# Reordering one stage border of a fused cross-attention and MLP kernel: the last G1 steps of batch 0, an activation-table load, and a W1 piece of batch 1

## The chip, the cores and the metric

The kernel runs on one core of one Trainium2 chip. A core has five engines that run their own instruction queues and meet only at semaphores: TensorE (PE in the profile, its weight loads PEld), VectorE (DVE), ScalarE (ACT), GpSimd (POOL) and SyncE (SP), which here only issues DMAs. The metric is the device time of one launch in microseconds (us), the median of several runs. Positions "at 36.55" are us from the start of the span in the profile of the kernel before.

## The reference, cut to what matters

```python
# x: (8, 8, 512, 64)  state: (8, 8, 32, 64)   B, H, S, D and B, H, Ns, D
scores  = (x @ state^T) / 8;      a  = softmax(scores);   xread = a  @ state    # 512 rows a batch
scores2 = (state @ x^T) / 8;      a2 = softmax(scores2);  sread = a2 @ x        # 32 rows a batch
t   = concat([xread, sread], axis=2)        # -> (8 * 544, 512), heads side by side
h   = t @ w_in                              # w_in (512, 2048)
out = (h * sigmoid(h)) @ w_out              # w_out (2048, 512), float32 result of 4352 x 512
```

The kernel leaves out the subtraction of the row maximum, which changes nothing in a softmax of such small scores.

## The kernel before, in words

**The algebra.** For the 512 x-rows of a batch `b`, `xread @ w_in` is `a @ (state @ w_in)`. So the kernel makes `W1[b] = state[b] @ w_in` (256 rows, one for each head and state, by 2048 columns) and multiplies the normalised softmax `aT[b]` with it; `xread` itself is never formed. The 32 sread rows of all eight batches are gathered and go through the MLP at the end as a "batch" 8 of their own.

**The steps of a batch, and their names.**
- `cast_x` converts x to bf16; `pe_transpose_x` (line 243) transposes it on TensorE through a PSUM bank, and a copy on the engine given in `engs` takes it to `xT`. Batches 0 and 1 do it this way; later batches use DMA transposes.
- `scores` (L304) and `exps` (L318): scores into PSUM, the exponential on ScalarE. `hg` 0 and 1 are the two halves of the heads.
- `norm` (L377 row sums, L378 reciprocal, both on VectorE; L380 product, on GpSimd for `hg` 0 and on VectorE for `hg` 1), then `pe_transpose_a` (L396): transposes the probabilities to `aT`.
- W1 in pieces of up to 512 columns: `w1_mms` (L464, eight small matmuls for each half of a PSUM pair) and `w1_out` (copies to bf16 `W1`, L156 on ScalarE or L158 on VectorE). A half-batch is one PSUM bank, so a 512-column piece needs two banks.
- G1 step `k` (L518, `emit_G1`): two matmuls of 512 columns, one for each `hg`, and a SILU on ScalarE (L550) that gives the tile `g` number `k`; batch `b` has the steps `16 b` to `16 b + 15`. `upto(n)` emits all steps below `n` that are not emitted yet. The two PSUM buffers of tag `h1` hold the G1 results, so step `k` cannot start before the SILU of step `k-2` has read its buffer.
- G2 (L559): one matmul of 512 columns that adds `g` number `ft` times `w_out` into one of the four output tiles `tt` of a batch; `store` copies a finished output tile to SBUF and writes it out.

**What sets the order.** The scheduler is switched off (`tc.manual_schedule()`); every engine runs its instructions in the order in which the program emits them, and a wait holds up all that stands behind it on its engine. The order around the change is written out by hand in lines 604 to 720. Lines 604 to 645 are the start: attention of batch 0, with dummy matmuls (`keep_busy`, L164) between. Lines 650 to 679 are a loop over `ft` 0 to 11 of batch 0 in which G1 runs `LEAD0[ft]` steps ahead (but not past `ready`, the W1 columns made so far), W1 pieces of batch 0 (`W0`) and batch 1 (`W1_AT`) are put in, and then G2 for `tt` 0 to 2, with some of `tt` 3. Lines 680 to 720 are the border to batch 1: the rest of G2 of batch 0 lies between the steps of the softmax of batch 1.

**Activation tables.** ScalarE holds one table at a time: the exponential and SILU take turns, with a table load between (`ACT_TABLE_LOAD`). Lines 686 and 700 are one-element activations (`warm`) that pull such a load to a chosen place: 686 ahead of the exponentials of batch 1, 700 back to SILU for its G1 steps.

**PSUM.** Eight banks: `o0`, `o1` (pool psO), two buffers `h1` (psH), `a0` to `a3` (psA). In batch 0 the output tiles `tt` 0 to 3 lie in `o0`, `o1`, `a0`, `a1`; `bank` gives the a-banks named in `banks` in turn, in the border only `a2` and `a3` at first.

The loop and the border of the kernel before, cut to what the change touches:

```python
    W0 = {2: (512, 512), 6: (1024, 512), 10: (1536, 512)}
    W1_AT = {4: 0, 6: 512, 10: 1024}
    LEAD0 = [2, 2, 2, 2, 2, 3, 2, 1, 3, 3, 2, 1]
...
    nc.scalar.activation(warm[:], busy[:, 0:1], func=EXP, bias=0.0)
    for ft in range(8, 11):
        G2(0, 3, ft)
    scores(1, 0, new=new_h)
    G2(0, 3, 11)
    scores(1, 1, new=new_h)
    exps(1, 0)
    exps(1, 1)
```

Of the kernel before, what the change touches and what calls it, by code (L numbers as in the profile page):

```python
# [14 lines left out]
EXP = mybir.ActivationFunctionType.Exp  # L15
# [26 lines left out]
def kernel(  # L42
# [8 lines left out]
    nc = tc.nc  # L51
# [14 lines left out]
    psO = ctx.enter_context(tc.tile_pool(name="psO", bufs=1, space=bass.MemoryType.PSUM))  # L66
    psH = ctx.enter_context(tc.tile_pool(name="psH", bufs=2, space=bass.MemoryType.PSUM))
    psA = ctx.enter_context(tc.tile_pool(name="psA", bufs=1, space=bass.MemoryType.PSUM))
# [38 lines left out]
    def load_x(b, h0=0, nh=H, eng=nc.gpsimd):  # L107
        eng.dma_start(
            x_f[b % 2][:, ds(h0, nh)],
            x[b, ds(h0, nh)].rearrange("h (p c) d -> p h c d", p=128, c=4)  # L110
        )
# [42 lines left out]
    def copy(eng, dst, src):  # L154
        if eng is nc.scalar:
            nc.scalar.activation(dst, src, func=COPY, bias=0.0)  # L156
        else:
            eng.tensor_copy(dst, src)  # L158


    def keep_busy(n, pool, tag):
        ps = pool.tile([128, 512], FP32, tag=tag, name="ps_busy")
        for _ in range(n):
            nc.tensor.matmul(  # L164
                ps[:], busy[:, 0:128], busy[:], start=True, stop=True, skip_group_check=True
            )

    warm = pers.tile([128, 1], FP32)
    busy = pers.tile([128, 512], BF16)
# [26 lines left out]
    both = (nc.vector, nc.scalar)  # L196
# [46 lines left out]
    def pe_transpose_x(b, hg, nb=2, new=bank, engs=(nc.vector, nc.scalar), only=None):  # L243
        if b not in xT:
            xT[b] = xtpool.tile([128, 4, 4, 128], BF16, tag="xT", name=f"xT{b}")
        m = 4 // nb
        for u in range(nb) if only is None else only:
            ps = new([128, m, 2, 128], BF16, "ps_xt")
            for i in range(m):
                for j in range(2):  # L250
                    nc.tensor.transpose(  # L251
                        ps[:, i, j, :],
                        x_nat[b][:, m * u + i, 2 * hg + j, :],
                        ident[:],
                    )
            copy(engs[u], xT[b][:, ds(m * u, m), ds(2 * hg, 2), :], ps[:])
# [41 lines left out]
    def scores(b, hg, m=4, new=bank):  # L298
        sc_ps[hg] = []
        for c in range(4):  # L300
            if c % m == 0:
                sc_ps[hg].append(new([128, m, 4, NS], FP32, "ps_sc"))
            for j in range(2):
                nc.tensor.matmul(  # L304
                    sc_ps[hg][-1][:, c % m, ds(2 * j, 2), :],
                    xT[b][:, c, 2 * hg + j, :],
                    stT[:, b, 2 * hg + j, :, :],
                    start=True,
                    stop=True,
                    skip_group_check=True,  # L310
                )
# [141 lines left out]
    def w1_mms(b, cols, new=bank):  # L453
        pss = {}
        if b not in W1:
            W1[b] = wpool.tile([128, 2, DF], BF16, tag="W1", name="W1")
        for f, n in cols:
            for hg in range(2):
                pss[f, hg] = new([128, 512], FP32, "ps_w1")
            for s in range(4):  # L460
                for hg in range(2):
                    h = HEAD_OF_SLOT[hg][s]
                    r = 64 * (h % 2)
                    nc.tensor.matmul(  # L464
                        pss[f, hg][ds(32 * s, 32), 0:n],
                        stT[ds(r, 64), b, h // 2, s % 2, :],
                        w_in_sb[ds(r, 64), h // 2, ds(f, n)],
                        start=True,
                        stop=True,
                        tile_position=(r, 32 * s),  # L470
                        skip_group_check=True,
                    )
        return pss

    def w1_out(b, cols, engs, pss, at=0):
        for f, n in cols:
            for hg in range(2):
                copy(engs[hg], W1[b][:, hg, ds(f + at, n)], pss[f, hg][:, ds(at, n)])

    def w1_cols(b, cols, engs, new=bank):  # L480
        w1_out(b, cols, engs, w1_mms(b, cols, new))
# [45 lines left out]
    def emit_G1(k):  # L527
        b, ft = divmod(k, NFT)
        if b < B:
            if k == 0:  # L530
                g1_first()
                return
            g1_half(k, 0)
            g1_half(k, 1)
            ps = h_ps.pop(k)
        else:
            ps = psH.tile([128, 512], FP32, tag="h1", name="h1")
            for kt in range(4):
                nc.tensor.matmul(  # L539
                    ps[:, 0:256],  # L540
                    w_in_sb[:, kt, ds(128 * ft, 128)],
                    xmT[:, :, kt].rearrange("p t n b -> p t (n b)"),
                    start=(kt == 0),
                    stop=(kt == 3),
                    skip_group_check=True,
                )
        n = 512 if b < B else 256
        g = gpool.tile([128, 512], BF16, tag="g", name="g")
        gt[k] = g
        nc.scalar.activation(g[:, 0:n], ps[:, 0:n], func=SILU, bias=0.0)  # L550

    def G2(b, tt, ft):
        if ft == 0:
            if b == 0 and tt >= 2:
                outs[tt] = psA.tile([128, DM], FP32, tag=f"a{tt - 2}", name="o_a")
            else:
                i = (tt + (b > 0)) % 2 if tt < 3 else 0
                outs[tt] = psO.tile([128, DM], FP32, tag=f"o{i}", name="o")
        nc.tensor.matmul(  # L559
            outs[tt][:],  # L560
            gt[b * NFT + ft][:, ds(128 * tt, 128)],
            w_out_sb[:, ft, :],
            start=(ft == 0),
            stop=(ft == NFT - 1),
            skip_group_check=True,
        )

    def store(b, tt, eng):
        o = opool.tile([128, DM], FP32, tag="o_sb", name="o_sb")
        copy(eng, o[:], outs[tt][:])  # L570
        if b < B:
            nc.sync.dma_start(out_re[ds(136 * b, 128), tt, :], o[:])
        else:
            nc.sync.dma_start(out_sread[ds(512, 32), ds(4 * tt, 4), :], o[:])
# [21 lines left out]
    def upto(k):  # L596
        while done[0] < min(k, (B + 1) * NFT):
            emit_G1(done[0])
            done[0] += 1

    new_h = lambda sh, dt, nm: psH.tile(sh, dt, tag="h1", name=nm)
# [2 lines left out]
    scores(0, 0)  # L604
    exps(0, 0)
    keep_busy(1, psH, "h1")
    pe_transpose_x(0, 1, 2, new_h, (nc.vector, nc.vector))
    norm(0, 0)
    scores(0, 1, 2)
    exps(0, 1)  # L610
# [38 lines left out]

    turn[0] = 0  # L650
    W0 = {2: (512, 512), 6: (1024, 512), 10: (1536, 512)}
    W1_AT = {4: 0, 6: 512, 10: 1024}
    LEAD0 = [2, 2, 2, 2, 2, 3, 2, 1, 3, 3, 2, 1]
    T3 = {1: (0, 1), 2: (2,), 3: (3,), 4: (4,), 5: (5,), 6: (6,)}
    ready = 4
    for ft in range(12):
        upto(min(ft + LEAD0[ft], ready))
        if ft == 1:
            place_one_state(1, transpose_one_state(st1_n), nc.vector)
        if ft in W0:  # L660
            pss = w1_mms(0, [W0[ft]])
            if ft in W1_AT:
                pss1 = w1_mms(1, [(W1_AT[ft], 512)], new_h)
            w1_out(0, [W0[ft]], both, pss)
            if ft in W1_AT:
                w1_out(1, [(W1_AT[ft], 512)], both, pss1)
            ready = sum(W0[ft]) // 128
        elif ft in W1_AT:
            w1_cols(1, [(W1_AT[ft], 512)], both)
        if ft == 11:  # L670
            for hg in range(2):
                cast_x(1, nc.vector, 0, 4, 4 * hg, 4)
            load_x(3)
        for tt in range(3):
            G2(0, tt, ft)
            if ft == 7 and tt == 0:
                upto(9)
        for i in T3.get(ft, ()):
            G2(0, 3, i)
    upto(14)  # L680
    G2(0, 3, 7)
    pe_transpose_x(1, 0, 1, engs=(nc.vector,))
    upto(15)
    pe_transpose_x(1, 1, 1, engs=(nc.vector,))
    upto(16)
    nc.scalar.activation(warm[:], busy[:, 0:1], func=EXP, bias=0.0)
    for ft in range(8, 11):
        G2(0, 3, ft)
    scores(1, 0, new=new_h)
    G2(0, 3, 11)  # L690
    scores(1, 1, new=new_h)
    exps(1, 0)
    exps(1, 1)
# [12 lines left out]
    G2(0, 3, 13)  # L706
    banks[:] = ["a2", "a3", "a0", "a1"]
    turn[0] = 0
    w1_cols(1, [(1536, 512)], (nc.vector, nc.vector))
    store(0, 1, nc.vector)  # L710
    for i in (2, 3):
        for c in range(4):
            cast_x(i, nc.gpsimd, c, 1)
# [108 lines left out]
```

The softmax here doesn't subtract the row's maximum and nothing guards it: scores larger than these inputs give would overflow.

## Time and profile before

| what | value |
| --- | --- |
| time, median of 3 runs | 216.12 us (216.08 to 216.12) |
| profiled span | 214.3 us, 3868 instructions |
| one 512-column matmul of G1 or G2, from one start to the next | 0.216 us (two take 0.43 us in the chain) |
| one SILU of 128 x 512 on ScalarE | 0.596 us |
| ACT_TABLE_LOAD | 1.283 us |
| W1 copy of 128 x 512, VectorE / ScalarE | 0.685 / 0.592 us |

The page of the profile gives busy times by engine, a strip of the span in 40 slices, DMA queues, the chain of work that ended last, and the costliest groups. The chain is read backwards from the last instruction: at each step it goes to what released that instruction, or to the instruction ahead of it on its engine. "Issue" is time in which the engine waited for nothing that the profile shows. The timeline lists instructions in order of time, merged while they are alike, and in square brackets the idle time of the engine ahead of an instruction and what ended it. The end of a matmul is modelled and overlaps the next by about 0.16 us, so on TensorE the distance from start to start is the thing to read.

### The profile page before, as it was taken

How to read it: one execution, taken by the hardware profiler on the slowest of the kernel's cores; microseconds unless marked ns; L12 is line 12 of the kernel's file. 1: busy time of each engine (PE TensorE's matmuls, PEld its weight loads, DVE VectorE, ACT ScalarE, POOL GpSimd, SP SyncE). 2: the span in 40 equal slices, each digit the busy share in tenths (PEclk: the TensorE clock that was granted, in tenths of full speed). 3: DMA queues.
4: the chain of work that ended last, by engine and by line, in shares of the span. 5: the costliest groups of instructions: out<-in, count | busy, mean ns of one | idle time of the engine just before them, and what ended most of it. 6: DMA issues, size and time to landing. Idle time of an engine off the chain costs nothing.

```text
span 214.3 us, 3868 instructions
## 1 busy us (share of the span) xinstructions
PE 205.3 (96%) x1549; PEld 97.0 (45%) x1575; DVE 76.7 (36%) x171; ACT 139.3 (65%) x244; POOL 39.9 (19%) x62
## 2 busy tenths in 40 slices
PE   7899998999899999999999999999999999999993
PEld 2443354445344444444444444444444444466653
DVE  3752275566951156106610651135312415200011
ACT  3766669699567876698559956886675366644410
POOL 8592213702420312003100402000200000000000
PEclk9999999999999999999999999999999999999999
DMA  6999999497649548464657483114310211011112
GB/s 200 191 205 206 292 268 345 123 251 246 83 97 272 159 109 195 98 198 104 180 68 245 77 178 100 49 52 104 97 50 22 85 49 54 0 49 49 52 49 98
DMA packets 42930, 28.66 MB, mean 134 GB/s; under 512 B 28064, under 2 KB 37792, under 8 KB 42912
## 3 DMA queue, kind: packets, MB, share of 16 engines
q1 hardware_dynamic: 36720, 20.65, 36.6%
q0 software_dynamic: 5904, 7.64, 17.2%
q8 instruction: 12, 0.20, 0.4%
q10 hardware_dynamic: 288, 0.13, 0.2%
q14 instruction: 6, 0.05, 0.1%
HBM read 17.43 MB, written 8.91 MB: 123 GB/s over the span
## 4 chain that ended last, share of the span: by engine, by line
PE 88%; DVE 6%; ACT 3%; issue 1%; POOL 0%
PE o L559 47%; PE h L518 25%; PE ps_w L464 4%; PE h L539 3%; PE o_a L559 2%; PE ps_busy L164 2%; PE o_part L581 2%; DVE rs L377 1%; DVE W L158 1%; PE ps_sr L416 1%; DVE rc L432 1%; PE ps_xt L251 1%; DVE an L380 1%; DVE xT L158 1%; ACT exp_nat L318 1%
## 5 line engine op out<-in xcount | busy, mean ns | idle before, releaser
L559 PE MATMUL o<-w_out_sb,g 128*128 128x512 bf16 x486 | 130.0, 379 | 1.7 <-issue 0.9
L550 ACT ACTIVATE g<-h 128x512 bf16<-128x512 f32 (+1 forms) x143 | 81.4, 573 | 36.9 <-PE h L518 21.8
L559 PEld LDWEIGHTS <-g 128*128 128x128 bf16 x528 | 50.2, 98 | 58.2 <-issue 3.5
L518 PE MATMUL h<-aT,W 128*128 128x512 bf16 x241 | 72.0, 379 | 0.1
L158 DVE COPY o_sb<-o 128x512 f32<-128x512 f32 x15 | 10.4, 691 | 87.7 <-PE o L559 80.2
L518 PEld LDWEIGHTS <-W 128*128 128x128 bf16 x254 | 24.5, 98 | 29.9 <-issue 1.0
L158 DVE CAST W<-ps_w 128x512 bf16<-128x512 f32 (+2 forms) x35 | 22.1, 658 | 26.4 <-PE ps_w L464 26.4
L156 ACT ACTIVATE W<-ps_w 128x512 bf16<-128x512 f32 (+1 forms) x33 | 17.1, 562 | 12.6 <-PE ps_w L464 12.6
L158 POOL CAST x_nat<-x_f 128x512 bf16<-128x512 f32 x24 | 14.6, 650 | 31.7 <-issue 21.7
L156 ACT ACTIVATE o_sb<-o 128x512 f32<-128x512 f32 x16 | 9.5, 596 | 12.1 <-PE o L559 8.9
L360 POOL TENSOR_TENSOR an<-e,rcn 128x512 bf16<-128x512 bf16 x5 | 7.6, 1518 | 51.0 <-DVE rcn L358 51.0
L464 PE MATMUL ps_w<-w_in_sb,stT 64*32 64x512 bf16 (+2 forms) x264 | 10.8, 375 | 0.8 <-DVE W L158 0.7
L539 PE MATMUL h<-xmT,w_in_sb 128*128 128x256 bf16 x64 | 9.6, 273 | 0.0
L559 PE MATMUL o_a<-w_out_sb,g 128*128 128x512 bf16 x30 | 9.6, 379 | 0.0
L539 PEld LDWEIGHTS <-w_in_sb 128*128 128x128 bf16 x64 | 6.3, 98 | 3.9
L164 PE MATMUL ps_busy<-busy 128*128 128x512 bf16 x15 | 6.4, 533 | 1.2 <-DVE warm L171 1.2
L766 ACT ACT_TABLE_LOAD x5 | 6.4, 1283 | 0.1
L344 ACT ACTIVATE eT<-ps_scT 128x512 bf16<-128x512 f32 x10 | 5.4, 595 | 1.6 <-PE ps_scT L330 1.6
L380 POOL TENSOR_TENSOR an<-exp_nat,rc 128x512 bf16<-128x512 bf16 x3 | 3.1, 1046 | 17.8 <-DMA x_f<-in_x_dram 10.6
L464 PEld LDWEIGHTS <-stT 64*32 64x32 bf16 x264 | 3.2, 89 | 7.0 <-issue 5.1
L357 DVE TENSOR_REDUCE rs<-e 128x32 f32<-128x1024 bf16 x5 | 6.1, 1211 | 0.6 <-DMA e<-eT 0.6
L432 DVE RECIPROCAL rc<-ps_sr 32x2 f32<-32x2 f32 x32 | 5.2, 164 | 0.3
(75 smaller groups left out, 104.1 us busy)
## 6 DMA issues: line engine op xcount, KB each, us to landing
out_dram<-o_sb SPq DMA_DIRECT2D x33, 256.0 KB, 2.4
x_f<-in_x_dram SPq DMA_DIRECT2D x4, 1024.0 KB, 5.8
x_f<-in_x_dram POOLq DMA_DIRECT2D x2, 1024.0 KB, 11.1
w_in_sb<-in_moe_w_in_dram POOLq DMA_DIRECT2D x3, 512.0 KB, 9.6
x_f<-in_x_dram SPq DMA_DIRECT2D x2, 512.0 KB, 4.7
w_out_sb<-in_moe_w_out_dram POOLq DMA_DIRECT2D x4, 256.0 KB, 11.5
w_out_sb<-in_moe_w_out_dram POOLq DMA_DIRECT2D x2, 512.0 KB, 11.4
x_f<-in_x_dram POOLq DMA_DIRECT2D x2, 512.0 KB, 14.2
```

The costliest lines, as they stand in the source:

```text
L156: nc.scalar.activation(dst, src, func=COPY, bias=0.0)
L158: eng.tensor_copy(dst, src)
L164: nc.tensor.matmul(ps[:], busy[:, 0:128], busy[:], start=True, stop=True, skip_group_check=True)
L357: nc.vector.tensor_reduce(rs[:], e2[b][:], axis=AX, op=ADD)
L360: eng.tensor_tensor(a[:, hg], e2[b][:, hg], rc[:, hg].to_broadcast([128, 4, 4, NS]), op=MULT)
L432: nc.vector.reciprocal(rc[q, :], src)
L464: nc.tensor.matmul(pss[f, hg][ds(32 * s, 32), 0:n], stT[ds(r, 64), b, h // 2, s % 2, :], w_in_sb[ds(r, 64), h // 2, ds(f, n)], start=True, ...
L518: nc.tensor.matmul(h_ps[k][:], W1[b][:, hg, ds(128 * ft, 128)], aT[b][:, hg, :, :], start=(hg == 0), stop=(hg == 1), skip_group_check=True,)
L539: nc.tensor.matmul(ps[:, 0:256], w_in_sb[:, kt, ds(128 * ft, 128)], xmT[:, :, kt].rearrange("p t n b -> p t (n b)"), start=(kt == 0), stop ...
L550: nc.scalar.activation(g[:, 0:n], ps[:, 0:n], func=SILU, bias=0.0)
L559: nc.tensor.matmul(outs[tt][:], gt[b * NFT + ft][:, ds(128 * tt, 128)], w_out_sb[:, ft, :], start=(ft == 0), stop=(ft == NFT - 1), skip_gr ...
L766: nc.scalar.activation(warm[:], busy[:, 0:1], func=SILU, bias=0.0)
```

## The change

It does three things.
- **At the start:** the second half of the second transpose of x of batch 0 (`hg` 1) is copied out of PSUM by ScalarE instead of VectorE, so the two copies can run side by side.
- **At the end of the loop of batch 0:** the last W1 piece of batch 0 is made alone at `ft` 10 (the W1 piece of batch 1 that stood beside it, columns 1024 to 1535, goes out). Then `ft` 11 emits the G1 steps 12 and 13 right away (lead 3), casts x of batch 1, transposes its first half, emits the steps 14 and 15 and asks for the exponential table, all ahead of the G2 steps of `ft` 11. The second transpose follows those G2 steps. It is meant to get ScalarE through with SILU of batch 0 earlier, so that the exponentials of batch 1 and what hangs on them come earlier.
- **In the border:** the two last W1 pieces of batch 1 are made in one group, all four banks copied out by VectorE. As four banks are needed at once, a list of its own (`tail_bank`) takes `a2`, `a3`, `a0` and `o0`, the latter two those of the output tiles 2 and 0 of batch 0, which ScalarE has stored by then. The store of output tile 1 moves ahead of the group.

```diff
-    pe_transpose_x(0, 1, 2, new_h, (nc.vector, nc.vector))
+    pe_transpose_x(0, 1, 2, new_h, both)
...
-    W1_AT = {4: 0, 6: 512, 10: 1024}
-    LEAD0 = [2, 2, 2, 2, 2, 3, 2, 1, 3, 3, 2, 1]
+    W1_AT = {4: 0, 6: 512}
+    LEAD0 = [2, 2, 2, 2, 2, 3, 2, 1, 3, 3, 2, 3]
...
             load_x(3)
+            pe_transpose_x(1, 0, 1, engs=(nc.vector,))
+            upto(16)
+            nc.scalar.activation(warm[:], busy[:, 0:1], func=EXP, bias=0.0)
         for tt in range(3):
             G2(0, tt, ft)
...
-    upto(14)
+    pe_transpose_x(1, 1, 1, engs=(nc.vector,))
     G2(0, 3, 7)
-    pe_transpose_x(1, 0, 1, engs=(nc.vector,))
-    upto(15)
-    pe_transpose_x(1, 1, 1, engs=(nc.vector,))
-    upto(16)
-    nc.scalar.activation(warm[:], busy[:, 0:1], func=EXP, bias=0.0)
-    for ft in range(8, 11):
+    scores(1, 0, new=new_h)
+    for ft in range(8, 12):
         G2(0, 3, ft)
-    scores(1, 0, new=new_h)
-    G2(0, 3, 11)
     scores(1, 1, new=new_h)
...
     turn[0] = 0
-    w1_cols(1, [(1536, 512)], (nc.vector, nc.vector))
+    tail_tags = ["a2", "a3", "a0", "o0"]
+
+    def tail_bank(shape, dtype, name):
+        tag = tail_tags.pop(0)
+        return (psO if tag == "o0" else psA).tile(shape, dtype, tag=tag, name=name)
+
     store(0, 1, nc.vector)
+    w1_cols(1, [(1024, 512), (1536, 512)], (nc.vector, nc.vector), tail_bank)
```

## The prediction

> **What bounds the kernel now.** I read the page first: which engine is busy, and whose work is the chain that ended last.
>
> ```profile
> PE 205.3 (96%) x1549; PEld 97.0 (45%) x1575; DVE 76.7 (36%) x171; ACT 139.3 (65%) x244; POOL 39.9 (19%) x62
> ...
> PE 88%; DVE 6%; ACT 3%; issue 1%; POOL 0%
> ```
>
> TensorE is busy for 96% of the span and is 88% of the chain. The change neither adds nor takes a matmul, so it can only win or lose where TensorE stands still. Second I asked the timeline of TensorE for gaps between 26 and 42 us, where the diff moves things:
>
> ```profile
> 36.55 0.40 PE L396 MATMUL ps_at<-ident,an 128*128 128x128 bf16 x4 [0.97 <-POOL an L380]
> 36.79 0.38 PE L559 MATMUL o_a<-w_out_sb,g 128*128 128x512 bf16 x1
> 37.10 0.40 PE L396 MATMUL ps_at<-ident,an 128*128 128x128 bf16 x4
> 37.65 0.41 PE L464 MATMUL ps_w<-w_in_sb,stT 64*32 64x512 bf16 x8
> 37.99 1.04 PE L518 MATMUL h<-aT,W 128*128 128x512 bf16 x4
> ...
> 40.58 0.59 PE L518 MATMUL h<-aT,W 128*128 128x512 bf16 x2
> ```
>
> The one real gap is ahead of 36.55. The twelve G2 steps before it started at 32.83; at 0.216 us they are through at 35.42, so 1.13 us are lost there. The second transpose, at 37.10, could have started at 36.79 + 0.216 = 37.00: 0.10 us more. What put the transpose at 36.55 is told by the chain in the same window:
>
> ```profile
> 31.70 0.60 ACT g L550
> ...
> 32.32 1.28 ACT L686
> ...
> 33.61 0.20 ACT warm L686
> 33.82 0.97 ACT exp_nat L318 x2
> 34.79 0.58 ACT o_sb L156
> ...
> 35.46 1.05 POOL an L380
> ...
> 36.55 0.40 PE ps_at L396 x4
> ```
>
> The last SILU of batch 0, the table load, the exponentials, the product on GpSimd. The step "o_sb" is the profile's guess: line 380 reads only exp_nat and the reciprocal rc. The timeline of VectorE has rc at 35.05 for 0.25, ending 0.16 us before GpSimd starts; the same 0.16 to 0.17 us lie there at 9.62 and 52.01. So the chain is exp, rs (34.33, 0.69), rc, product, and it hangs on the table load at 32.32.
>
> Third, the start of the kernel, in the chain:
>
> ```profile
> 7.83 0.76 DVE xT L158 x2
> 8.59 0.61 DVE rs L377
> ...
> 9.47 0.61 DVE rs L377 x2
> ...
> 10.38 0.84 DVE an L380
> ...
> 11.94 0.49 PE h L502 x3
> ```
>
> and in the timeline of ScalarE:
>
> ```profile
> 8.64 0.71 ACT L318 ACTIVATE exp_nat<-ps_sc 128x256 bf16<-128x256 f32 x2 [0.65 <-PE ps_sc L304]
> ```
>
> Here VectorE is the chain: two copies of xT, then everything of the softmax, while ScalarE has 0.65 us free ahead of 8.64 (its exponential at 7.39 ends at 7.99).
>
> **What the Trainium skill says.** "ScalarE: Activation LUTs", section What ACT_TABLE_LOAD costs: about 1283 ns for the load and about 1380 ns of drain. The load agrees (1.28 us); the drain does not show here: warm starts at 33.61, right behind the load, and the exponential at 33.72. I use 1.40 us from load to exponential. The same section gives an ACTIVATE with immediates 186 ns + 0.833 ns an element, 612 ns for 512, whatever the type; the trace has 0.384 for 256 and 0.591 to 0.597 for 512. "PSUM — Partial Sum Buffer", section Engine vs sequencer instructions: the queues of ScalarE, VectorE and GpSimd are strictly first in, first out. The trace agrees: every engine follows the program text, so a moved line really moves all that stands behind it.
>
> **Part 1, the copy at the start.** The trace has no 128x512 bf16 PSUM copy on ScalarE. Bounds: 0.59 us (its 512-column rows) and 0.63 us (its cast of x); I take 0.60. The second four transposes end near 8.02, so the copy runs 8.04 to 8.65, where VectorE ended the same copy at 8.59: the second half of the scores comes 0.05 us later, the last exponential ends at 9.39 instead of 9.35, and this costs nothing else on ScalarE (table load at 9.75 instead of 9.71). On VectorE, rs starts at 8.16 instead of 8.50, rc at 8.87, the first half sum at 9.04, the second at 9.41 (it waits for that exponential; before 9.68), rc at 9.83, product at 10.11 instead of 10.38. Gain 0.27 us; bounds 0 and 0.34 (the copy's whole step). It reaches TensorE: the dummy matmuls end near 10.5, the transpose that waited for the product moves from 11.28 to 11.01, ScalarE's part of aT (11.2 to 11.6) is in time for L502 at 11.67. No load catches it: the nearest, the w_in columns from 512, landed at 5.0 + 9.6 = 14.6 and are used at 15.52; the one of columns 1536 at 12.2 + 13.1 = 25.3, used at 26.80.
>
> **Part 2, the loop's end,** on the clock of before (all of it 0.27 earlier if part 1 holds). TensorE at 26.80: eight W1 matmuls instead of sixteen, 0.34 instead of 0.56 us (the eight are added back in part 3). Three G2 steps to 27.79. G1 step 12 needs the new W1 piece: at `ft` 2 the same order took 1.23 us from the first W1 matmul (15.52) to G1 (16.75), so step 12 starts at 28.03. **A new wait of 0.24 us**, with G1 12 to 15 and the table load queued behind it. Steps 12, 13 to 28.90; eight transposes to 29.34 (the cast of x ends at 28.6 for this half; its second half waits for x at 28.2 and ends at 29.25, with only the xT copy behind it on VectorE); step 14 to 29.77. Step 15 waits for the SILU of 13: SILU starts 0.64 us after the first matmul of a pair of steps (37.99 to 38.63), so 28.67, and the second ends at 29.75: step 15 at 29.80 to 30.23. Its SILU runs 30.52 to 31.12; the table load comes at **31.13 instead of 32.32**. TensorE: three G2 to 30.88, transposes to 31.32, one G2, scores (xT was copied by 30.2), four G2, scores, at 32.86: where it was before (32.83). Twelve G2 to 35.45.
>
> ScalarE: exponentials at 31.13 + 1.40 = 32.53 and 33.07. VectorE and GpSimd keep their distances, 1.19 us earlier: product on GpSimd ends at 35.3, on VectorE at 35.85. TensorE reaches the first transpose at 35.45, after the product: **the 1.13 us are gone**, with 0.1 to 0.15 us to spare. G2 to 35.90; the second transpose finds its product just ready: 0 to 0.05 lost. G2, and W1 at 36.46.
>
> **Part 3, the border.** Sixteen W1 matmuls, 0.56 us: to 37.02. Their banks are free: a2 and a3 since the xT copies (32.2), o0 and a0 with the stores on ScalarE, which follow the G2 steps and not the exponentials, and end by 35.4 and 35.9. G1 16 needs aT (copied by 36.8), so it starts at 37.02 instead of 37.99. ScalarE's SILU table: load behind those stores at 35.9, ready at 37.4; the first SILU is wanted at 37.66. From G1 16 to G1 20 the trace has 2.59 us, which the SILUs set; kept, 20 starts at 39.61 instead of 40.58. Gain **0.97 us**, less 0 to 0.1 for the tight product: 0.93. VectorE: the store of tile 1 (36.75 to 37.4) ahead of G2 of batch 1 at 39.2; then four copies at 0.645 us to 40.0, where before two copies and a store ended at 40.01. They cost nothing on the path: G1 24 wants the columns from 1024 near 42.2, G1 28 those from 1536 near 44.8. The state transposes wait on SP for the store of tile 1 and get earlier too. From 41.2 on TensorE is solid, and the later steps hang on each other, not on a clock.
>
> **Sum:** 0.27 + 0.93 = 1.20; 216.12 - 1.20 = **214.9 us**.
>
> **Rivals.**
> - *Both parts hold* (0.55): 214.9, 214.7 to 215.1 with the bounds of the copy (0 to 0.34) and the tight product.
> - *Only the border gains* (0.17): the copy on ScalarE pushes the exponentials behind it, and VectorE then waits for them. For it: it takes the same 0.65 us gap almost whole. 216.12 - 0.93 = 215.2.
> - *A wait in place of the one removed* (0.13): step 12 or the SILUs of 12 to 15 come later by half a us (x landing at 28.2, buffers h1), and the product is late again by that much: 216.12 - 0.6 = 215.5. Against: the cast of the first half does not need the late load, and the SILU distances are measured.
> - *No change* (0.07): the chain to the product keeps its place, the front gain pays for the new wait: 216.1.
> - *Slower* (0.08): neither gain, the 0.24 us at step 12 are new: 216.36; and if VectorE's two additional copies (1.29 us) hold up its work for batch 2, up to 217. For it: VectorE carries the whole group of four. Against: it has 3.1 us idle ahead of 43.73.
>
> **Range and chances.** Low 214.5: the 214.7 above, and 0.2 if the SILU-bound stretch of G1 16 to 20 also loosens. High 215.7, which takes in the first three cases. Faster by over 0.2%: 0.85; within: 0.07; slower: 0.08.
>
> **What would show it.** In the profile after: no gap over 0.1 us ahead of the L396 transposes of batch 1; table load of the exponential about 1.2 us (with the front 1.45) earlier; 0.2 us of wait at G1 12 for a DVE copy of W; one group of sixteen L464 near 36.2; L502 near 11.67; the product of batch 0 on VectorE near 10.1. I am wrong if TensorE waits anew at G1 14 or 15, for GpSimd at the transpose, or for VectorE around G1 24, or if the gain at G1 20 is lost again by 60 us.

## The result, and the profile after

The changed kernel takes 214.8 us (median of four runs, 214.54 to 215.1) against 216.1 us before: a ratio of 0.994, 95% interval 0.9923 to 0.9958. Run again beside experiments it took 214.71 us against 216.06 (0.9938, 0.9923 to 0.9952).

For the reading, three marks on TensorE are enough. **S** is the start of the second group of x transposes of batch 0 (L251), the last thing ahead of the copy that the change moves. **M** is the first matmul of the last W1 group of the loop (26.80 us before). **G1 20** is the fifth G1 step of batch 1 (40.58 us before). From S to M only the front part can act, from M to G1 20 only the border part; some of the expectations call this second distance D.

First the page. TensorE's share of the span rose from 96 to 97%, and its share of the chain from 88 to 90%:

```profile
span 212.8 us, 3896 instructions
...
PE 206.4 (97%) x1575; PEld 96.6 (45%) x1575; DVE 77.0 (36%) x171; ACT 139.4 (66%) x244; POOL 39.9 (19%) x62
...
PE 90%; DVE 4%; DMA 2%; ACT 2%; issue 0%; SPq 0%
```

Its higher busy time is not more work: the program has as many matmuls as before (PEld counts 1575 weight loads in both), and the trace of before has 1549 of them, that of after all 1575.

The timeline of TensorE in the border. A row gives the start and the length. A bracket would give the idle time that is left behind the modelled end of the matmul ahead, and there is none in the whole stretch; a shorter wait shows only in the distance from start to start:

```profile
26.24 0.41 PE L464 MATMUL ps_w<-w_in_sb,stT 64*32 64x512 bf16 x8
...
27.02 0.38 PE L559 MATMUL o_a<-w_out_sb,g 128*128 128x512 bf16 x1
27.46 1.04 PE L518 MATMUL h<-aT,W 128*128 128x512 bf16 x4
...
34.47 0.59 PE L559 MATMUL o<-w_out_sb,g 128*128 128x512 bf16 x2
34.90 0.39 PE L396 MATMUL ps_at<-ident,an 128*128 128x128 bf16 x4
35.12 0.38 PE L559 MATMUL o_a<-w_out_sb,g 128*128 128x512 bf16 x1
35.34 0.39 PE L396 MATMUL ps_at<-ident,an 128*128 128x128 bf16 x4
...
35.87 0.63 PE L464 MATMUL ps_w<-w_in_sb,stT 64*32 64x512 bf16 x16
36.43 1.04 PE L518 MATMUL h<-aT,W 128*128 128x512 bf16 x4
...
39.01 0.59 PE L518 MATMUL h<-aT,W 128*128 128x512 bf16 x2
```

The 0.97 us of idle time ahead of the first L396 row are gone: the two transposes start at 34.90 and 35.34, each just when the G2 steps ahead of it are through (34.47 + 0.43 and 35.12 + 0.22). M to G1 20 is 39.01 - 26.24 = 12.77 us; before it was 40.58 - 26.80 = 13.78. Next, ScalarE, GpSimd and VectorE in the timeline of all engines:

```profile
30.52 1.28 ACT L676 ACT_TABLE_LOAD   x1
...
31.92 1.19 ACT L318 ACTIVATE exp_nat<-ps_sc 128x512 bf16<-128x512 f32 x2
...
33.65 1.04 POOL L380 TENSOR_TENSOR an<-exp_nat,rc 128x512 bf16<-128x512 bf16 x1 [3.73 <-DVE rc L378]
...
34.37 0.88 DVE L380 TENSOR_TENSOR an<-exp_nat,rc 128x512 bf16<-128x512 bf16 x1
```

Counted from M, the table load stands at 4.28 us instead of 5.52. GpSimd's product is ready at 34.69, and TensorE only comes for it at 34.90. The profile now also names the reciprocal rc as the releaser, not the store that it named before.

The start, in the timeline:

```profile
7.17 0.61 PE L251 MATMUL ps_xt<-ident,x_rows 128*128 128x128 bf16 x8
7.59 0.43 DVE L158 COPY xT<-ps_xt 128x512 bf16<-128x512 bf16 x1 [0.46 <-PE ps_xt L251]
7.82 0.60 ACT L156 ACTIVATE xT<-ps_xt 128x512 bf16<-128x512 bf16 x1
7.93 0.68 DVE L377 TENSOR_REDUCE rs<-exp_nat 128x16 f32<-128x512 bf16 x1
...
9.05 1.05 POOL L380 TENSOR_TENSOR an<-exp_nat,rc 128x512 bf16<-128x512 bf16 x1 [2.06 <-DVE rc L378]
...
9.95 0.70 DVE L380 TENSOR_TENSOR an<-exp_nat,rc 128x512 bf16<-128x512 bf16 x1
...
11.37 0.20 PEld L502 LDWEIGHTS <-W 128*128 128x128 bf16 x2 [0.27 <-issue]
```

The two copies (7.59 on VectorE, 7.82 on ScalarE) run side by side. From S (7.17) to the second L502 weight load it is 4.20 us; before it was 11.94 - 7.41 = 4.53. But M came 0.56 us earlier than in the first profile of before, which is more than these 0.33: S itself stood 0.24 us earlier, and nothing ahead of S was changed. That asked for an experiment.

### The profile page after: what moved, and what is told of

Its sections match the earlier page's. It is cut to its first block, busy times and chain, and to the rows that moved or that the text cites. A ratio compares the mean times of both kernels' runs of the same rounds, so it can differ in the third digit from the quotient of the medians.

```text
span 212.8 us, 3896 instructions
## 1 busy us (share of the span) xinstructions
PE 206.4 (97%) x1575; PEld 96.6 (45%) x1575; DVE 77.0 (36%) x171; ACT 139.4 (66%) x244; POOL 39.9 (19%) x62
## 4 chain that ended last, share of the span: by engine, by line
PE 90%; DVE 4%; DMA 2%; ACT 2%; issue 0%; SPq 0%
PE o L559 48%; PE h L518 26%; PE ps_w L464 4%; PE h L539 3%; PE o_a L559 3%; DMA x_f<-in_x_dram 2%; PE o_part L581 2%; DVE W L158 1%; PE ps_sr L416 1%; DVE rc L432 1%; PE ps_scT L330 1%; PE ps_busy L164 1%; ACT L318 1%; DVE rs L377 1%; ACT exp_nat L318 1%; PE ps_at L396 0%
## 5 line engine op out<-in xcount | busy, mean ns | idle before, releaser
L559 PE MATMUL o<-w_out_sb,g 128*128 128x512 bf16 x496 | 132.2, 379 | 0.0
L518 PE MATMUL h<-aT,W 128*128 128x512 bf16 x254 | 74.7, 379 | 0.1
L158 DVE CAST W<-ps_w 128x512 bf16<-128x512 f32 (+2 forms) x36 | 22.7, 658 | 26.3 <-PE ps_w L464 26.3
L156 ACT ACTIVATE W<-ps_w 128x512 bf16<-128x512 f32 (+1 forms) x32 | 16.6, 561 | 12.6 <-PE ps_w L464 12.6
L464 PE MATMUL ps_w<-w_in_sb,stT 64*32 64x512 bf16 (+2 forms) x264 | 10.8, 375 | 0.7 <-DVE W L158 0.7
L164 PE MATMUL ps_busy<-busy 128*128 128x512 bf16 x16 | 5.9, 487 | 1.2 <-DVE warm L171 1.2
L380 POOL TENSOR_TENSOR an<-exp_nat,rc 128x512 bf16<-128x512 bf16 x3 | 3.1, 1047 | 15.7 <-ACT eT L344 9.9
## 6 DMA issues: line engine op xcount, KB each, us to landing
x_f<-in_x_dram POOLq DMA_DIRECT2D x2, 512.0 KB, 14.6
```

The lines of the kernel that those rows point to most:

```text
L164: nc.tensor.matmul(ps[:], busy[:, 0:128], busy[:], start=True, stop=True, skip_group_check=True)
L464: nc.tensor.matmul(pss[f, hg][ds(32 * s, 32), 0:n], stT[ds(r, 64), b, h // 2, s % 2, :], w_in_sb[ds(r, 64), h // 2, ds(f, n)], start=True, ...
L518: nc.tensor.matmul(h_ps[k][:], W1[b][:, hg, ds(128 * ft, 128)], aT[b][:, hg, :, :], start=(hg == 0), stop=(hg == 1), skip_group_check=True,)
L559: nc.tensor.matmul(outs[tt][:], gt[b * NFT + ft][:, ds(128 * tt, 128)], w_out_sb[:, ft, :], start=(ft == 0), stop=(ft == NFT - 1), skip_gr ...
```

## The experiments

My theory was that of the prediction: two independent gains, one in the start and one in the border, and in the border one cause, the place of the G1 steps ahead of the table load. The rivals were that the start's gain is luck, that the W1 piece or the explicit table request does it, and that the new wait at G1 step 12 could have been avoided.

### The two halves alone, and both kernels again

The first kernel has one line of the change, the second all the others:

```diff
 front only, on the kernel before
-    pe_transpose_x(0, 1, 2, new_h, (nc.vector, nc.vector))
+    pe_transpose_x(0, 1, 2, new_h, both)

 border only, on the changed kernel
-    pe_transpose_x(0, 1, 2, new_h, both)
+    pe_transpose_x(0, 1, 2, new_h, (nc.vector, nc.vector))
```

> The kernel before with the one edit at the start: ScalarE copies the second half of the second transpose of x of batch 0. My theory: the softmax chain of batch 0 on VectorE gets 0.27 us shorter (0 to 0.34), so the first matmul of the last W1 piece of batch 0 starts near 26.5 instead of 26.80 and the time is about 215.8. From that matmul to G1 step 20 the distance stays 13.78 us. Rival: the 0.56 us that the profile of the changed kernel shows at that mark is luck of the start of that one execution (the clock of TensorE, the landing of x) and has nothing to do with the copy: time 216.1, mark at 26.8.

> The changed kernel with the copy at the start put back on VectorE. My theory: the border alone brings what it brought together with the front: from the last W1 group of the loop to G1 step 20 12.8 us instead of 13.78, time 215.1 to 215.2, and as steady as the kernel before (spread under 0.1). Rival: the border needs the earlier start or shares its gain with it: time 215.5 or more. A third: the spread of 0.56 us between the runs of the changed kernel comes from the border, then it is seen here too.

> The changed kernel once more, for a second profile of it beside the two halves on the same chip. My theory: median 214.8, runs from 214.5 to 215.1; the border again 12.8 us from the last W1 group to G1 step 20, and the start between 26.2 and 26.6 at that W1 group: the spread sits in the first 12 us. Rival: the start is the same 26.24 and the spread sits later.

> The kernel before, one more look at its start. If the first 8 us differ from its first profile in the pace of the transposes and dummy matmuls on TensorE between 4.4 and 6.6, the start of each execution has its own luck; the mark at 26.80 should not move by more than 0.1, since its times lie within 0.05 us. Rival: the mark moves by some 0.3 us as in the changed kernel.

| kernel | time, us | ratio to before | S | S to second L502 load | M | M to G1 20 |
| --- | --- | --- | --- | --- | --- | --- |
| before, first profile | 216.12 | | 7.41 | 4.53 | 26.80 | 13.78 |
| before, again | 215.88 | | 7.17 | 4.54 | 26.58 | 13.77 |
| front only | 215.67 | 0.9977 (0.9966 to 0.9988) | 7.71 | 4.20 | 26.78 | 13.78 |
| border only | 215.15 | 0.9951 (0.9933 to 0.997) | 7.16 | 4.55 | 26.57 | 12.78 |
| changed | 214.8 | 0.994 (0.9923 to 0.9958) | 7.17 | 4.20 | 26.24 | 12.77 |
| changed, again | 214.71 | 0.9938 (0.9923 to 0.9952) | 7.19 | 4.21 | 26.42 | 12.77 |

The two gains are independent and add up: against 216.06 us in that series the front alone brings 0.39, the border alone 0.91, both 1.35. In the columns of distances it is sharper: 0.33 us from S to L502 and 1.0 us from M to G1 20, each only where its half of the change is in.

The other columns tell where most of the spread comes from. S wanders from 7.16 to 7.71 us with no regard to the change, and what the program does ahead of S is the same in all six profiles: it waits for x to land (its first cast on ScalarE starts between 4.97 and 5.27) and runs the first transposes. So my expectation that the mark at 26.80 would be steady in the kernel before was wrong: in its second profile it is 26.58. With the front alone it is 26.78 and not near 26.5, as S was late there (7.71). Nor does the border alone run within 0.1 us: its runs lie between 214.82 and 215.40. One part of the spread lies later. From S to M it is 19.39 to 19.41 us in the three profiles without the front and 19.07 in two with it, but 19.23 in the second profile of the changed kernel; a load of `w_in` is the reason (below, "No load catches it"). So a single profile of such a kernel must be read in distances, not in places.

### The request for the table

```diff
             upto(16)
-            nc.scalar.activation(warm[:], busy[:, 0:1], func=EXP, bias=0.0)
```

> The changed kernel without the one-element exponential that asks for the table behind G1 step 15; the load is left to the exponentials themselves. D is the distance on TensorE from the first matmul of the last W1 group of the loop to G1 step 20: 13.78 us before, 12.77 after. My theory: a load waits for nothing, and ScalarE takes its queue in order, so it comes right behind the SILU of step 15 in either case: D 12.77, time 214.7. What brings the load early is the place of the G1 steps. Rival: without the request the load stays with the exponential and waits with it for the scores, 0.8 us later; then the product is late and D is 13.3, time 215.2.

It took 214.82 us, M to G1 20 is 12.78. ScalarE's timeline of this run:

```profile
31.05 1.28 ACT L318 ACT_TABLE_LOAD   x1
32.35 1.29 ACT L318 ACTIVATE exp_nat<-ps_sc 128x512 bf16<-128x512 f32 x2
```

M is at 26.77 here, so the load comes 4.28 us behind it, just where it comes with the request. It does not wait for the input of its exponential: the scores start on TensorE only at 31.51 in this run, 0.46 us after the load. So the request does no work at this place. It even holds up the first exponential a little: without it that starts 1.30 us behind the start of the load, with it 1.40. Nothing hangs on this 0.1 us here, the distance is 12.78 and 12.77. The rival falls.

### The G1 steps 14 and 15 put back

```diff
             pe_transpose_x(1, 0, 1, engs=(nc.vector,))
-            upto(16)
-            nc.scalar.activation(warm[:], busy[:, 0:1], func=EXP, bias=0.0)
         for tt in range(3):
...
     pe_transpose_x(1, 1, 1, engs=(nc.vector,))
     G2(0, 3, 7)
+    upto(16)
+    nc.scalar.activation(warm[:], busy[:, 0:1], func=EXP, bias=0.0)
     scores(1, 0, new=new_h)
```

> The changed kernel with G1 steps 14 and 15 and the request for the table put back behind the second transpose of x and the G2 step that follows it; the lead of steps 12 and 13 and the W1 group of two pieces stay. My theory: ScalarE gets to the table load some 1.3 us later, GpSimd's product is late again, TensorE waits about 1.1 us ahead of the first transpose of the probabilities, D is 13.8 and the time 215.7. Rival: the gain comes from the W1 piece or from the steps 12 and 13, and D stays near 12.9.

It took 216.09 us (ratio 0.9988, 0.9977 to 0.9999): with these two steps late nearly the whole gain is gone, and the border is worse than before (M at 26.58, G1 20 at 40.64: 14.06 us). The timeline of TensorE:

```profile
31.71 0.39 PE L304 MATMUL ps_sc<-stT,xT 128*128 128x64 bf16 x8 [0.25 <-ACT g L550]
...
36.41 0.40 PE L396 MATMUL ps_at<-ident,an 128*128 128x128 bf16 x4 [0.62 <-POOL an L380]
```

The wait for GpSimd is back, as expected, and with it the cause is shown: the request alone moved nothing in the run above, so it is the place of these two steps. (The early steps 12 and 13 were not tried alone.) The other wait I had not expected: the scores take a G1 buffer, and right behind G1 14 and 15 both buffers still wait for their SILUs, so TensorE stands 0.25 us ahead of the scores. It costs nothing: the exponential starts 1.40 us behind its table load all the same (32.17 and 33.57), and TensorE waits for the product afterwards. That the distance is 14.06 and not 13.8 has another reason, which I had not counted: the eight W1 matmuls that the change moved now stand behind the wait for the product and not ahead of it. From the first transpose to G1 16 it is 1.64 us here and 1.44 before. The rest is the product itself, 8.72 us behind M instead of 8.66.

### The W1 piece: left in place, and moved alone

```diff
 left in place, on the changed kernel
-    W1_AT = {4: 0, 6: 512}
+    W1_AT = {4: 0, 6: 512, 10: 1024}
...
-    w1_cols(1, [(1024, 512), (1536, 512)], (nc.vector, nc.vector), tail_bank)
+    w1_cols(1, [(1536, 512)], (nc.vector, nc.vector), tail_bank)

 moved alone, on the kernel before (with tail_tags and tail_bank as in the change)
-    W1_AT = {4: 0, 6: 512, 10: 1024}
+    W1_AT = {4: 0, 6: 512}
...
-    w1_cols(1, [(1536, 512)], (nc.vector, nc.vector))
-    store(0, 1, nc.vector)
+    store(0, 1, nc.vector)
+    w1_cols(1, [(1024, 512), (1536, 512)], (nc.vector, nc.vector), tail_bank)
```

> The changed kernel with the W1 piece of batch 1 (columns 1024 to 1535) left where it was, beside the last piece of batch 0; all else as in the change. My theory: this piece lies in the two PSUM buffers of G1, so G1 step 12 must wait for its copies on VectorE and ScalarE: it starts 1.80 us after the first W1 matmul instead of 1.22. The chain to the product moves with it, and TensorE too; the eight matmuls missing later give 0.22 back: D 13.1, time 215.05. Rival: the place of the piece is neutral, or better, since its eight matmuls fill the 0.24 us that step 12 waits: D 12.55 to 12.77.

> The kernel before with nothing but the W1 piece of batch 1 moved into one group of four banks with the last piece, all copied by VectorE, store of tile 1 ahead of it. My theory: TensorE reaches the transposes 0.22 us earlier and waits longer there, the chain over the table load gets 0.22 earlier, the eight matmuls come back behind it: D 13.78, time 216.05, no change. Rival: VectorE's two additional copies hold something up: D or the time over 216.3. Other rival: the move by itself brings part of the gain: D 13.55 or less.

Moved alone the piece is worth nothing: 216.04 us (ratio 1.0001, 0.9987 to 1.0015), 13.78 us from M (26.84) to G1 20 (40.62). Four copies in a row on VectorE hold up nothing, so that rival falls, and so does the one that the move alone brings part of the gain.

Left in place it costs 0.2 us of the border's gain: 215.13 us, and 12.97 from M (26.64) to G1 20 (39.61). The timeline of TensorE:

```profile
26.64 0.62 PE L464 MATMUL ps_w<-w_in_sb,stT 64*32 64x512 bf16 x16
...
28.29 1.02 PE L518 MATMUL h<-aT,W 128*128 128x512 bf16 x4 [0.27 <-ACT W L156]
```

G1 step 12 starts 1.65 us behind M instead of 1.22, and waits for ScalarE's copy of this W1 piece. The mechanism is the expected one, a PSUM buffer of G1 held by W1, but 0.15 us smaller than I worked out (1.80): the releaser is ScalarE's second copy, which ends at 28.24, and I had taken VectorE's, which ends at 28.41. The chain comes 0.43 us later, and the eight matmuls that are then missing behind it give 0.22 back. So the move is no gain by itself; it makes room for the early G1 steps.

### G2 steps in the waits that are left

Two waits are left in the border after the change: 0.22 us ahead of G1 12 (27.46 against 27.02 + 0.216 = 27.24 above), and 0.2 us spread over G1 16 to 20. Each is about one G2 step long.

```diff
 filled, on the changed kernel
-    T3 = {1: (0, 1), 2: (2,), 3: (3,), 4: (4,), 5: (5,), 6: (6,)}
+    T3 = {1: (0, 1), 2: (2,), 3: (3,), 4: (4,), 5: (5,), 6: (6,), 10: (7,)}
...
     pe_transpose_x(1, 1, 1, engs=(nc.vector,))
-    G2(0, 3, 7)

 spread, on the changed kernel
     pe_transpose_a(1, 1, nc.vector, new_h)
-    G2(0, 3, 13)
...
     upto(NFT + 2)
+    G2(0, 3, 13)
     G2(0, 3, 14)
-    G2(0, 3, 15)
     upto(NFT + 3)
+    G2(0, 3, 15)
```

> The changed kernel with one G2 step (output tile 3, number 7) moved from behind the second transpose of x to the end of round 10 of the loop, ahead of G1 step 12. My theory: G1 step 12 waits there for the copy of its W1 columns, 0.24 us by my prediction, and a G2 step of 0.216 us fills that wait. The chain to the product does not move, TensorE reaches the first transpose 0.2 us earlier and finds the product just ready: D 12.55 to 12.7, time 214.5 to 214.65. Rival: the product then comes late by as much and D stays 12.77.

> The changed kernel with the G2 steps of output tile 3 spread otherwise: number 13 goes from between the second transpose of the probabilities and the W1 group to behind G1 step 17, and number 15 from ahead of G1 step 18 to behind it. My theory: the 2.59 us from G1 16 to G1 20 are set by the SILUs, which leave TensorE idle for 0.2 us; with one G2 step more between them it is not idle: D 12.57, time 214.5. Rival: G1 16 cannot start earlier, since it waits for the copy of the probabilities or ScalarE for its table; then D stays 12.77.

> Both of these moves together. My theory: they add up, D 12.4, time 214.35. Rival: with TensorE 0.4 us earlier the product on GpSimd or ScalarE's SILU table is what comes last, and only one of the two gains is left: D 12.6.

> The kernel with both moves of G2 steps, and without the one-element exponential that asks for the table. My theory: with the first move alone the products came last (the second transpose started 0.05 us behind VectorE's product), so what shortens the chain to the products gives time again. Without the request the exponentials start 1.30 us behind the table load instead of 1.40, as the run without it showed; so D is 0.1 us below the two moves together: 12.45 against 12.55, and the time 214.3. Rival: something else came last there, and D stays 12.55.

| kernel | time, us | ratio to before | M | G1 20 | M to G1 20 |
| --- | --- | --- | --- | --- | --- |
| filled | 214.73 | 0.9939 (0.9926 to 0.9952) | 26.46 | 39.22 | 12.76 |
| spread | 214.35 | 0.9924 (0.9911 to 0.9936) | 26.40 | 38.97 | 12.57 |
| filled and spread | 214.55 | 0.9941 (0.9921 to 0.9961) | 27.87 | 40.42 | 12.55 |
| the same, no table request | 214.7 | 0.9934 (0.9912 to 0.9956) | 26.48 | 38.95 | 12.47 |

*Filled* is a miss of mine, and the rival says why. The wait at G1 12 is filled, but G1 12 itself still starts 1.22 us behind M (27.68), since it waits for the copy of its W1 columns; so the chain that it begins, over the SILUs and the table load to the products, is no shorter. TensorE reaches the transposes of the probabilities earlier, and waits there for the products, all engines in one timeline:

```profile
33.88 1.04 POOL L380 TENSOR_TENSOR an<-exp_nat,rc 128x512 bf16<-128x512 bf16 x1 [2.98 <-DVE rc L378]
34.60 0.88 DVE L380 TENSOR_TENSOR an<-exp_nat,rc 128x512 bf16<-128x512 bf16 x1
...
34.98 0.40 PE L396 MATMUL ps_at<-ident,an 128*128 128x128 bf16 x4
...
35.53 0.23 PEld L396 LDWEIGHTS <-an 128*128 128x128 bf16 x4 [0.27 <-DVE an L380]
```

VectorE's product ends at 34.60 + 0.88 = 35.48, and the second transpose starts at 35.53. In the changed kernel that transpose came 9.10 us behind M, here 9.07. So the 0.22 us at G1 12 cost nothing that a filler could win, since the chain over the table load ends right behind.

*Spread* won what was expected, 0.20 us from M to G1 20, and TensorE no longer stands among G1 16 to 20: with the G2 steps between them they start at 36.37, 37.68, 38.32 and 38.97 (16 and 17 together, then 18, 19, 20), each a whole number of 0.216 us matmuls behind the one ahead. *Filled and spread* kept only that one gain, as the rival had it (the profile is of an execution whose start was late, M at 27.87, so only the distance is used). The last kernel then took 0.1 us off the chain to the products by leaving out the table request, and the distance fell by 0.08, to 12.47: what had come last was that chain.

By the times alone these four can't be told from one another or surely from the changed kernel: the intervals of the ratios overlap, and the wandering start is as large as the differences. By the distance, the last one is 0.3 us shorter than the changed kernel and the spread one 0.2.

## Why the prediction was right

The prediction was 214.9 us, the time 214.8, and the likeliest case, both parts, is what happened. By its steps:

- **What bounds the kernel.** Right: the gain is TensorE's idle time, and nothing else. From G1 20 to the end of the span it is 173.7 us before (214.3 - 40.58) and 173.8 after (212.8 - 39.01); nothing was given back later, as the prediction wanted for the stretch from 41.2 on.
- **The chain behind the gap.** Right: the table load was to come 1.19 us earlier and came 1.24 earlier, counted from M, and the products moved with it. That the profile's "o_sb" was a wrong guess held too: the first store starts 7.99 us behind M in the changed kernel (34.23) and 7.96 before, yet GpSimd's product starts 7.41 us behind M (33.65), ahead of that store, instead of 8.66.
- **The new wait at G1 12.** Right in size, 0.22 against 0.24 us. The experiment that filled it shows that a filler wins nothing there: the W1 copy ahead of G1 12 is part of the chain to the products.
- **The time to spare at the transposes.** 0.21 us at the first instead of the 0.1 to 0.15 expected, none lost at the second. So the 0.04 us that were taken off for a tight product were not needed, and the border gained 1.01 instead of 0.93.
- **The W1 group.** Right: it started 9.63 us behind M, 9.66 was worked out. Banks and the four copies on VectorE (2.47 us) cost nothing, and moved alone the piece changes nothing.
- **The start.** Right in kind, but the sum was wrong in two terms of opposite sign, so that it came as near as it did in part by luck. It took VectorE's own chain as the limit, the second row sum waiting for the second exponential, and a gain of 0.27 us. That chain gained only 0.19: counted from S, VectorE's product began at 2.97 before and at 2.78 after. But the product also took 0.70 us instead of 0.83, and this the prediction left out. VectorE's product ends 0.55 us behind GpSimd's wherever the two overlap (last section), and GpSimd's product, which needs only the first half of the row sums, began the whole 0.33 us earlier (1.88 us behind S instead of 2.21). So 0.33 us reached L502, close to the bound of 0.34.
- **"No load catches it".** This step held in most executions, not in all. The prediction named the loads of columns 512 and 1536; the one of columns 1024 was left out. In the changed kernel's second profile and in the filled one TensorE waits for it. Weight loads of the former:

```profile
20.05 0.75 PEld L559 LDWEIGHTS <-g 128*128 128x128 bf16 x4
21.22 0.14 PEld L464 LDWEIGHTS <-stT 64*32 64x32 bf16 x16 [0.42 <-DMA w_in_sb<-in_moe_w_in_dram]
```

The bracket of 0.42 us stands there without a wait too, then put down to "issue"; it is the distance that tells. In the first profile this group starts 3.03 us behind the W1 group ahead of it (18.01 to 21.04), here 3.19 (18.03 to 21.22), and from S to M the two executions lose 0.16 and 0.18 of the 0.33 us. The reason is a slow load: it landed 10.8 us after its issue in these two, 9.2 to 10.3 in the other twelve profiles. It is not simply that TensorE is too early: the load is issued right behind GpSimd's product and moves with it, so that from its issue to the group it is 10.99 us before (10.62 to 21.61) and after (10.05 to 21.04). Whether an early issue makes a slow landing more likely stays open.

What the early start did use up is the margin of the load of columns 512, which is issued at 5.0 us in every profile and does not move. It landed at 14.6 and was used at 15.52 before; in the changed kernel it landed at 5.02 + 9.8 = 14.8 and was used at 14.95. No wait shows yet: its group starts 7.78 or 7.79 us behind S in all profiles with the front but the late one. But a start that is earlier still could meet this load.

The rival "only the border gains" is refuted by the front alone (0.39 us), "a wait in place of the one removed" by the transposes that start right behind the G2 steps ahead of them, and "slower" by the time itself and by the W1 piece moved alone.

## What to carry to other kernels

Here the table load came right behind what stood ahead of it in ScalarE's queue, and did not wait for the input of its exponential; a request just ahead of that exponential moved nothing. The place in the queue does count: the load back to SILU stands behind the two stores (34.23 and 34.73 in the changed kernel) and starts only at 35.34. So to get an exponential earlier, move the producers of the activations ahead of it earlier in TensorE's order, and let TensorE's work that nobody waits for fill the time behind. Then check what a buffer of the moved steps is shared with: here W1 in a G1 buffer cost 0.2 us. And where the start of an execution wanders by half a microsecond, compare distances between marks around the edit: M to G1 20 repeats to 0.02 us for a kernel where the times do not.

## What the hardware did that I had not expected

- VectorE's product (L380, 128 x 512 bf16) takes 0.70 us at the start of the changed kernel, 0.83 before and 0.88 in the border, though it is the same instruction. GpSimd's product of the other half of the heads runs at the time. The pair at the start of the kernel before, and that of the late execution (filled and spread), where the two do not overlap:

```profile
9.62 1.05 POOL L380 TENSOR_TENSOR an<-exp_nat,rc 128x512 bf16<-128x512 bf16 x1 [2.66 <-ACT W L156]
10.38 0.83 DVE L380 TENSOR_TENSOR an<-exp_nat,rc 128x512 bf16<-128x512 bf16 x1
...
10.43 1.05 POOL L380 TENSOR_TENSOR an<-exp_nat,rc 128x512 bf16<-128x512 bf16 x1 [3.19 <-DVE rc L378]
...
11.59 0.69 DVE L380 TENSOR_TENSOR an<-exp_nat,rc 128x512 bf16<-128x512 bf16 x1
```

Alone it takes 0.69 us. Where the two overlap, by 0.15 us (start of the changed kernel), 0.29 (before), 0.33 (border) or 0.36 (batch 2), VectorE's ends 0.55 us behind GpSimd's, in all 41 such pairs of the fourteen profiles (0.54 to 0.55). So, as an estimate from these numbers, an overlap of up to 0.14 us (0.69 - 0.55) is free, and what lies beyond it makes the product longer by as much. The Trainium skill ("GPSIMD Engine Reference", section Specifications) says that GpSimd shares its SBUF interfaces with VectorE and contends with VectorE instructions of two SBUF inputs, which this product is. The numbers fit that, but no run here changed the overlap alone, and that the interfaces are the cause is not shown.
- The drain behind a table load that the skill prices ("ScalarE: Activation LUTs", section What ACT_TABLE_LOAD costs) did not show in any run: without the request the exponential started 1.30 us after the start of the 1.28 us load.
- The start of an execution differs by up to half a microsecond, once by over one, with the same instructions: S lay between 7.16 and 7.71 us in all profiles but the late one (filled and spread), where it was 8.30 and its eight transposes took 1.06 us instead of 0.61.
